# Wider key-value products and denominators in a four-layer attention kernel

## The chip, the cores and the metric

The kernel runs on one core of one Trainium2 chip. The metric is the device time of one execution in microseconds (us). Times below are a median of three runs; the profile is one more execution, read with the hardware profiler.

## The reference

Four residual blocks follow each other on x of 2048 rows by 512 columns: A, B, A, B, the two A with the same weights and the two B as well. Each block normalizes its input, projects it to queries, keys and values of 32 heads with 16 columns each, and ends with a projection by wo. A is attention in a causal window of 256 rows with a softmax; B is linear attention over all rows, whose denominator is one number per row and head.

```python
    def _B_ref(x, wqkv, wo):
...
        phi = lambda t: jnp.where(t > 0, t + 1, jnp.exp(t)) + 1e-6
        pq, pk = phi(q), phi(k)
        kv = jnp.einsum("bhsd,bhse->bhde", pk, v)
        z = jnp.einsum("bhsd->bhd", pk)
        num = jnp.einsum("bhqd,bhde->bhqe", pq, kv)
        den = jnp.einsum("bhqd,bhd->bhq", pq, z)[..., None] + 1e-6
        o = num / den
        return (lambda x, *d: x.transpose(*d))(o, 0, 2, 1, 3).reshape(B, S, D) @ wo

    x = A_x
    x = x + _A_ref(_layernorm(x, axis=-1), A_wqkv, A_wo)
    x = x + _B_ref(_layernorm(x, axis=-1), B_wqkv, B_wo)
    x = x + _A_ref(_layernorm(x, axis=-1), A_wqkv, A_wo)
    x = x + _B_ref(_layernorm(x, axis=-1), B_wqkv, B_wo)
```

## The kernel before

The rows lie in 16 tiles of 128 and in 4 groups I of 4 tiles. The program has two rounds, a = 0 and a = 1, each of one A and one B block. Within a round, group I runs through LayerNorm and transposes (`ln_tile`), the A projections (`prep`: keys, queries, values), scores, exponentials, masks and products with the values (`attention`), the output of A (`out_A`), LayerNorm again, and the B projections (`b_proj`). After the last group, `kv_final` makes what the second half of B needs; that half, `norm_p2`, runs while the next round's A has begun, and for a = 1 it ends the program.

In B each tile's phi(k) and v give a product of 512 columns of phi(k) by 33 columns (32 of v and a 1), split in 16 blocks of 32 rows of the result. `kv_unit` does two tiles at a time: 32 matmuls, each with 32 weight columns, which go to four column groups of the array, into one PSUM bank; VectorE then adds the bank to the running sum `kvs`. The denominators are made by `norm_pair(h)` for two groups I at once: 8 matmuls (L1072) with 64 weight columns from `zc` and 512 moving columns of phi(q), in two column groups of 64; then ScalarE takes Ln and Exp of -1 times that, one engine copies the reciprocals to bf16 (`hl`), and VectorE adds the rest in the other rows. `norm_unit` spreads them to the columns of each head (L1097) and VectorE multiplies phi(q) with them (L1101); `p2_tile` projects with `wkv`, the key-value product already multiplied with wo.

A transpose (`transpose`, L553) is done either on TensorE (four matmuls against the identity, L568, and a copy out of PSUM, L571) or by a DMA from the SP queue (L559). `by_pe` says which. Two sums of check flags (`check_layer`) multiply one column of flags as the weights with a column of ones.

The order of all work is written out by hand in the string `ORDER` (L214): each word is an operation's number, the engine that does it (P TensorE, A ScalarE, V VectorE, G GpSimd, S the SP queue) and the buffers that it takes; the planner emits them in that order. A word such as `9F0` puts matmuls without use into a bank (`fill`, L464) where TensorE would stand idle. Operations whose cost names more than one engine can stand on either; masks, copies out of PSUM, LayerNorm's parts and phi's middle step are of this kind.

```python
        for t in range(NCT):
            k_unit(key, I, t)
            q_unit(key, I, t)
```

For I = 0 the keys and queries come in halves (`k_half`, `q_half`): half 0 needs the transposed tiles 0 and 1, half 1 the tiles 2 and 3.

Of the kernel before, what the change touches and what calls it, by code (L numbers as in the profile page):

```python
# [10 lines left out]
ALU = mybir.AluOpType  # L11
# [208 lines left out]
130P 131P 99V 163P04 344V1 164A 102P3 162G 132V 165A 188P06 638V0 348G 141P4 189A 142P 143P 144P 119S 154P5 103V 166G  # L220
155P 156P 190A 145V 157P 193P02 13G 158V 345P4 194A 340P6 167P7 349V0 168P 639G 169P 346V 170P 195A 171V 199P04 11G
646V1 200A 31S 110P2 12G 355P7 111V 201A 341V 1F3 204P02 192G 650V2 381P6 43S 647G 205A 350P5 382P 351V 203G 206A 356V
198G 210P04 640V12 32H 363P7 383V 30H 641S 211A 364P 209G 191G 365V 212A 2F3 224P02 651G 108P6 172S0 225A 385P4 109V
196G 386P 197G 213V 226A 384S 229P06 207V 202G 387V 214P5 215P 230A 648V1 216P 208G 360P4 652V3 642V0 231A 217P 235P02
361P 653S 218V 643G 236A 357P7 362V 358P 228G 237A 649S 644V0 233G 240P04 359V 219P6 241A 220P 221P 645S 222P 238V 242A
947V0 246P02 389P7 390P 247A 223V 245G 388S 227G 391V 248A 2F5 397P04 232V 234G 239G 1F6 668P7 398A 249V 948G 669P 244V
250P6 392S 399A 670V 402P02 251P 671V 403A 252P 401G 253P 939V1 243G 393P7 404A 407P04 254V 940G 394P 176S1 408A 366P6
395V 367P 943V2 409A 412P02 396S 255P7 368V 256P 413A 944G 257P 258P 411G 682P6 414A 259V 418P04 400G 683P 410V 419A
264S2 416V 661P7 415G 684V 662P 420A 405V 434P02 417G 663V 260S3 369P6 435A 422V 370P 421G 664V 654P5 41S 406G 436A 655P
423V 371V 424P4 439P20 437G 425P 51S 276V 441A 429P6 430P 656V 426P 440A 431P 657V 427P 33S 432P 428V 444P02 372P7 445A  # L230
433V 373P 47S 446A 374V 449P04 378P6 951V3 686P7 450A 447G 34H 49S 687P 448V 952G 438V 451A 941V00 455P02 379P 688V 442G
456A 679P5 37S 380V 454G 680P 453G 443V 457A 452V 471P06 681V 35S 473A 459V 458G 3F4 476P24 460V 953V1 472A 461P7 466P6
689S 462P 477A 474V 467P 475G 463P 468P 478A 464P 36H 469P 465V 481P02 173P5 480G 39S 482A 479V 470V 174P 483A 175V
486P06 375P4 685S 180V1 376P 487A 485G 377V 181G 488A 2F5 492P20 40H 694P5 42H 695P 493A 48H 949V3 489G 50H 954S 945V2
658P7 490V 659P 494A 696V 177P6 942S 491V 508P42 484V 660A 496V 495G 178P 509A 497V 498P7 179V 697S 499P 510A 500P
513P04 184V0 503P6 514A 504P 501P 505P 515A 502V 506P 518P02 507V 261P7 519A 517G 262P 690P6 520A 263V 523P04 691P 511V
524A 265P7 692V 266P 525A 516V 529P02 693S 267V 530A 521V 2F6 665P5 528G 527V 522G 666P 526V 531A 698P06 667V 512G 675P4
185G 950S 699A 676P 532V 534V 533V 677V 700A 2F5 703P20 45S 540P5 268V2 541P 704A 535P7 701V 542P 269G 536P 705A 946S
543P 537P 544V 538P 708P02 706G 539V 672P6 702G 46H 709A 557S0 182G01 44H 673P 678V 52H 38H 710A 674V 713P04 979P7 553S1
980P 714A 711G 976P6 712G 981V 549S2 715A 719P02 270G1 977P 720A 717V 545S3 958P4 718G 959P 978V 721A 716G 955P5 707V  # L240
960V 735P06 956P 737A 723V 722G 982S 724V 957V 730P4 736A 740P62 731P 272V1 732P 741A 725P5 726P 273G 727P 742A 728P
733P 739G 745P60 734V 546P2 744G 746A 729V 554P3 555P 747A 577V 750P64 556V 547P 751A 748G 743V 983P3 548V 984P 752A
756P06 569V2 757A 755G 985V 738G 749V 758A 986S 5F2 772P42 753V 754G 773A 760V 3F1 777P06 759G 761V 8V 778A 767P4 762P5
183S 768P 774A 763P 769P 764P 779A 271S 770P 765P 782P02 766V 961P7 781G 783A 274G2 780V 962P 771V 558P6 784A 963V
787P04 275S 559P 788A 785G 967P3 560V 775G 968P 789A 786V 793P06 776G 991P2 969V 794A 992P 792G 791V 795A 993V 2F5
809P40 790V 810A 797V 2F3 814P26 798G 796V 186G0 561V1 815A 799P5 804P4 800P 811A 562G 805P 187S 801P 806P 816A 802P
813V 563G32 807P 803V 819P02 964P7 820A 808V 570G 965P 550P6 817G 821A 966V 824P04 551P 825A 823V 319P7 822V 320P 552V
826A 830P02 321V 331P6 831A 812V 332P 829G 828V 313P7 827G 333V 832A 314P 995P04 818G 315V 996A 834G 835V 2F6 1000P62
833V 1002A 565V0 836P1 841P0 837P 573V1 997A 842P 838P 843P 1001A 839P 998G 844P 840V 1006P24 566G 322A0 987P7 571V0
846S3 1007A 988P 1005G 845V 325P6 567G1 1008A 989V 326P 1011P02 323V 1003G 970P7 327V 1012A 850S1 574G 971P 973P6 1013A  # L250
972V 1017P04 858S0 974P 324V 1018A 1016G 847P7 975V 1004G 848P 994S 1019A 1031P02 1015G 1014V 282P60 849V 1032A 1020G
283P 878V 859P7 1033A 999G 862V0 1036P04 854S2 860P 1037A 1009V 863G 277P21 861V 1021P3 572S 278P 1038A 1010V 284V 1022P
1026P7 1035V 279A 1023P 1039G 1024P 334A2 575G2 280V 1042P04 1025V 290P61 1043A 281V 1027P 335G 576S 291P 874V1 1044A
1028P 1047P02 1029P 990S 1049A 285P50 336V 286P 1048A 855P4 1030V 856P 292V 864G20 287A 1053P02 851P7 564S 1040V 1054A
288V 852P 1051G 289V 295P62 1055A 568S 296P 875G 857V 293P5 297A 1050V 1034G 1083P02 294V 303P40 1046V 1085A 298V 300P51
1041G 853V 301P 1056G 1084A 299V 304P 1052G 308P70 870V0 302A 1057P6 305A 1088P02 1045V 871G 578P51 1090A 306V 1058P
307V 579P 1089A 872G0 1059P 309P 1060P 310A 1062P4 873S 1061V 1094P02 580A 311P7 1096A 1063P 312V 583P60 866V0 1064P
1095A 584P 581V 1065P 582V 316A0 1099P02 1098G 632P7 1066V 867G 1101A 633P 585V 1067S0 876G3 586P52 1100A 634V 587P
591P41 317V 868G1 588A 1105P02 626P7 589V 1107A 1091V 592P 1102G 869S 318V 627P 1097G 1106A 590V 1068P6 1069P 1092V 865S
# [90 lines left out]
def build(ctx, tc, A_x, A_wqkv, A_wo, B_x, B_wqkv, B_wo, out, force_safe=False):  # L350
# [94 lines left out]
    def fast_network(ctx_f):  # L445
# [62 lines left out]
        for k in range(3):  # L508
            nc.vector.memset(vss[k][:, :, 32:33], 1.0)
# [928 lines left out]
```

## Time and profile before

| | |
|---|---|
| median of 3 runs | 422.84 us (422.48 to 422.93) |
| the profiled execution | 423.23 us |
| its span, first to last instruction | 421.4 us |
| granted TensorE clock, mean | 0.998 |
| instructions | 15390 |

The profiled execution is 1.83 us longer than its span and 0.39 us above the median. In the page, a line's busy time is a union over the instructions of an engine. In the chain of waits, each piece is the time by which that work moved the end on, so a piece can be shorter than the instruction in it; "issue" is time in which the engine waited for nothing that the profile shows.

### The profile page before, as it was taken

The numbers are of one execution on the slowest core, as the hardware profiler recorded it, in microseconds if no ns is written. First come the engines' busy times: TensorE is split into PE (matmuls) and PEld (weight loads), VectorE is DVE, ScalarE is ACT, GpSimd is POOL, SyncE is SP. The second block draws the span as 40 slices with busy tenths as digits, with TensorE's granted clock in tenths as the row PEclk, the third lists the DMA queues.
The fourth block names the chain that finished last, engine by engine and source line by source line (L and its number), as shares of the span: only waits on it lengthen the run. The fifth ranks groups of instructions, "written<-read, shape, count | busy, mean of one in ns | idle before, by whom it ended". The sixth has DMA issues, their size and how long they took to land.

```text
span 421.4 us, 15390 instructions
## 1 busy us (share of the span) xinstructions
PE 398.1 (94%) x6281; PEld 221.1 (52%) x6355; DVE 360.9 (86%) x868; ACT 363.3 (86%) x485; POOL 237.0 (56%) x500
## 2 busy tenths in 40 slices
PE   7989999999999999999999999999999999999994
PEld 3665555555555555643555555555555556564341
DVE  6899898877889897988988999989778799888993
ACT  4999989999999999576998999999999999955630
POOL 4687633363757763353895566675645449433541
PEclk9999999999999999999999999999999999999999
DMA  7333273151203230100022123122213202210023
GB/s 232 119 82 77 66 196 80 38 99 29 40 16 66 52 63 16 29 2 0 5 64 54 39 48 63 42 52 64 52 28 54 52 16 54 39 26 2 2 81 124
DMA packets 64219, 23.86 MB, mean 57 GB/s; under 512 B 45072, under 2 KB 64144, under 8 KB 64144
## 3 DMA queue, kind: packets, MB, share of 16 engines
q1 hardware_dynamic: 62080, 21.38, 23.0%
q10 hardware_dynamic: 2064, 1.44, 1.1%
q8 instruction: 51, 0.84, 0.8%
q14 instruction: 24, 0.20, 0.1%
HBM read 6.29 MB, written 2.10 MB: 20 GB/s over the span
## 4 chain that ended last, share of the span: by engine, by line
PE 52%; ACT 18%; DVE 16%; issue 7%; DMA 2%; POOL 2%; another core or an unknown queue 0%; SPq 0%; DVEq 0%; ACTq 0%; POOLq 0%
PE psb L539 31%; PE psb L882 11%; ACT pt L839 9%; ACT pt L836 7%; PE psb L825 7%; DVE pqT L1101 2%; DVE pt L854 2%; DMA wA<-in_A_wqkv_dram 2%; DVE kall L775 2%; DVE qT L529 1%; DVE kall L790 1%; PE psb L568 1%; POOL pt L859 1%; PE psb L997 1%; DVE o_sb L896 1%
## 5 line engine op out<-in xcount | busy, mean ns | idle before, releaser
L859 POOL TENSOR_SCALAR_AFFINE_SELECT pt<-pt 128x256 bf16<-128x256 bf16 x279 | 116.5, 447 | 101.3 <-ACT pt L839 70.2
L836 ACT ACTIVATE pt<-psb 128x1024 bf16<-128x1024 f32 (+2 forms) x156 | 156.6, 1008 | 9.0 <-PE psb L825 7.8
L839 ACT ACTIVATE pt<-psb 128x1024 bf16<-128x1024 f32 (+2 forms) x156 | 156.6, 1011 | 3.8 <-PE psb L825 1.8
L882 PEld LDWEIGHTS <-pt 128*128 128x128 bf16 x2880 | 83.0, 96 | 19.0 <-issue 5.6
L882 PE MATMUL psb<-vbd,pt 128*128 128x34 bf16 x2880 | 87.5, 178 | 2.5 <-ACT pt L836 0.6
L539 PE MATMUL psb<-xnT,wA 128*128 128x512 bf16 (+1 forms) x306 | 65.3, 335 | 2.1 <-issue 0.5
L825 PE MATMUL psb<-qT,kall 32*128 32x256 bf16 (+4 forms) x1664 | 63.5, 241 | 2.5 <-ACT pt L836 0.8
L539 PE MATMUL psb<-wB,xnT 128*128 128x512 bf16 x230 | 62.0, 379 | 2.1 <-issue 1.1
L854 DVE TENSOR_TENSOR pt<-pt,tri 128x256 bf16<-128x256 bf16 (+1 forms) x138 | 52.7, 404 | 4.3 <-ACT pt L839 3.0
L825 PEld LDWEIGHTS <-kall 32*128 32x128 bf16 x1664 | 28.7, 92 | 47.7 <-issue 43.0
L539 PEld LDWEIGHTS <-xnT 128*128 128x128 bf16 x384 | 32.2, 97 | 35.8 <-issue 6.7
L539 PEld LDWEIGHTS <-wA 128*128 128x128 bf16 x320 | 27.7, 97 | 24.9 <-issue 6.5
L539 PE MATMUL psb<-wA,xnT 128*128 128x512 bf16 x112 | 32.5, 380 | 2.4 <-DMA wA<-in_A_wqkv_dram 0.9
L539 PE MATMUL psb<-woA,oT 128*128 128x512 bf16 x118 | 32.9, 380 | 1.0 <-issue 0.5
L539 PE MATMUL psb<-xnT,wB 128*128 128x512 bf16 x123 | 33.3, 379 | 0.4 <-issue 0.2
L539 PE MATMUL psb<-wkv,pqT 128*128 128x512 bf16 (+1 forms) x129 | 31.0, 373 | 0.9 <-DVE pqT L1101 0.5
L896 DVE TENSOR_TENSOR o_sb<-psb,rall 128x256 bf16<-128x256 f32 x64 | 27.2, 425 | 2.3
L895 DVE RECIPROCAL rall<-psb 128x16 f32<-128x16 f32 x64 | 16.1, 251 | 14.1 <-PE psb L882 11.1
L663 DVE BATCH_NORM_STATS2 ln<-xres 128x6 f32<-128x512 f32 (+1 forms) x39 | 26.6, 682 | 1.3 <-DMA xres<-in_A_x_dram 1.1
L950 ACT ACTIVATE pks<-psb 128x512 bf16<-128x512 f32 x32 | 19.4, 614 | 5.9 <-PE psb L539 5.8
L598 POOL TENSOR_TENSOR ln<-ln,mhalf 128x1 f32<-128x1 f32 x36 | 21.0, 582 | 3.0
L956 DVE SCALAR_TENSOR_TENSOR pks<-psb,pks 128x512 bf16<-128x512 f32 x32 | 22.0, 687 | 0.6
(129 smaller groups left out, 525.4 us busy)
## 6 DMA issues: line engine op xcount, KB each, us to landing
vbd<-vst SPq DMA_DIRECT2D x128, 34.0 KB, 1.9
wB<-in_B_wqkv_dram SPq DMA_DIRECT2D x6, 256.0 KB, 3.8
out_dram<-ost SPq DMA_DIRECT2D x10, 128.0 KB, 2.0
xres<-in_A_x_dram SPq DMA_DIRECT2D x4, 256.0 KB, 3.1
xnT<-xn SPq DMA_TRANSPOSE x48, 2.5
out_dram<-ost ACTq DMA_DIRECT2D x5, 128.0 KB, 1.7
wA<-in_A_wqkv_dram SPq DMA_DIRECT2D x1, 512.0 KB, 7.3
xres<-in_A_x_dram SPq DMA_DIRECT2D x1, 512.0 KB, 8.3
```

The source lines that it names most:

```text
L539: nc.tensor.matmul(t["t"][:], lhsT=lhs(c), rhs=rhs(c), start=(c == 0), stop=(c == NCT - 1))
L598: nc.gpsimd.tensor_tensor(out, out, mhalf[:, 0:1], op=ALU.pow)
L663: nc.vector.bn_stats(t["st"], x())
L825: nc.tensor.matmul(psb[:, sT.k + x if x < 2 else sS.k + x - 2, at * 64:(at + w) * 64], lhsT=kbd[half(m)][32 * x:32 * x + 32, tt, m % 4, :, :],
L836: nc.scalar.activation(body[:, 0:2, 0:w_all, :], psb[:, sT.k:sT.k + 2, 0:w_all * 64].rearrange("p x (s c) -> p x s c", c=64), ACT.Exp, sca ...
L839: nc.scalar.activation(body[:, 2:4, 0:w_all, :], psb[:, sS.k:sS.k + 2, 0:w_all * 64].rearrange("p x (s c) -> p x s c", c=64), ACT.Exp, sca ...
L854: nc.vector.tensor_tensor(v, v, mt, op=ALU.mult)
L859: nc.gpsimd.affine_select(out=v, in_=v, compare_op=ALU.is_ge, fill=0.0, base=1 if kind == 0 else -2, pattern=[[0, 4], [2 * sg, 64]], chann ...
L882: nc.tensor.matmul(t["O"][:, x, g, :, :], lhsT=parts[b][0][:, s0:s0 + 2, :], rhs=vbd[half(m)][:, m % 4, :, 4 * tt + g, :], start=(n == 0), ...
L896: nc.vector.tensor_tensor(o_sb[:, u0:u0 + nu, P * tt:P * tt + P].rearrange("p u (h e) -> p u h e", e=DH), Ov[:, :, :, 0:DH], r.to_broadcas ...
L950: nc.scalar.activation(dst(), ps()[:], ACT.Exp)
L956: nc.vector.scalar_tensor_tensor(out=dst(), in0=ps()[:], scalar=1.0 + 1e-6, in1=dst(), op0=ALU.add, op1=ALU.max)
```

## The change

1. `kv_unit` does four tiles at once (64 matmuls) for I = 0, 1, 2 and two at a time only for I = 3: 10 units in place of 16, of the same 512 matmuls in all, and 10 copies or additions of `kvs` in place of 16. The buffers of phi(k) and v grow from 3 to 5.
2. `zc` gets 32 columns in place of 64; a denominator's 8 matmuls go to four column groups of 32, which can stand in the array at once, two matmuls summed in each.
3. The sums of flags have a column of ones spread to 128 weight columns, and the flags as the moving column.
4. In round a = 1, group 0, tiles 2 and 3 are transposed by DMA and no longer on TensorE.
5. `kvn` and `hl` have no buffers of their own any more and use those of phi(k).
6. One landing time that the order was planned with (`wA`, values) is 9.5 in place of 8.6, and `ORDER` is new as a whole: fills 50 in place of 45, 60 in place of 68 copies by `evac` on VectorE and 32 in place of 24 on ScalarE, 28 in place of 20 LayerNorm applications on VectorE and 11 in place of 19 on GpSimd.

```diff
-7V 3G 6G 1G 14H 53V3 15H 0G 9G 58V2 17H 54A 5G 55V00 2G 59A 68A1 9F0 56P6 60V2 18H 19H 16H 63V0 61P4 57V 62V 64A 3F1
...
-                 "pks": Ring(3), "vs": Ring(3), "ln": Ring(4)}
+                 "pks": Ring(5), "vs": Ring(5), "ln": Ring(4)}
...
-        kvn = fp.tile([P, NCT, P], BF, name="kvn")
-        zc = fp.tile([P, NCT, 2, 2, DH], BF, name="zc")
+        zc = fp.tile([P, NCT, 2, DH], BF, name="zc")
...
-                nc.tensor.matmul(t["p"][:], lhsT=t["ok"][:], rhs=ones_bf[:], start=True, stop=True)
-            o2 = pl.op({"PE": .1}, f2, deps=[o], take=[s])
+                nc.tensor.matmul(psb[:, s.k, 0:1], lhsT=ones_bf[:].to_broadcast([P, P]), rhs=t["ok"][:], start=True, stop=True)
+            o2 = pl.op({"PE": .03}, f2, deps=[o], take=[s])
...
-        def kv_unit(i):
+        def kv_unit(i, tiles):
...
-                        for n in range(2):
+                        for n in range(tiles):
...
-                for c in range(NCT):
+                for n in range(2):
                     for k in range(2):
-                        nc.tensor.matmul(psb[64 * k:64 * k + 64, s.k, :], lhsT=zc[:, c, :, :, :],
-                                         rhs=pqT[:, c, (2 * h + k) * 512:(2 * h + k + 1) * 512],
-                                         start=(c == 0), stop=(c == NCT - 1), tile_position=(0, 64 * k))
+                        for q in range(2):
+                            c, r = 2 * q + n, 64 * k + 32 * q
+                            nc.tensor.matmul(psb[r:r + 32, s.k, :], lhsT=zc[:, c, :, :], rhs=pqT[:, c, (2 * h + k) * 512:(2 * h + k + 1) * 512],
+                                             start=(n == 0), stop=(n == 1), tile_position=(0, r))
...
-                if u % 2:
-                    kv_unit(4 * I + u - 1)
+                if u == 3 and I < NI - 1:
+                    kv_unit(4 * I, 4)
+                elif u % 2 and I == NI - 1:
+                    kv_unit(4 * I + u - 1, 2)
...
-                    ln_tile(ka, 4 * I + u, a == 0, by_pe=I == 0 or I == 1 and a == 0)
+                    ln_tile(ka, 4 * I + u, a == 0, by_pe=I == 0 and (a == 0 or u < 2) or I == 1 and a == 0)
```

Line numbers after the change are 1 lower up to L930, and up to 12 higher from L1041 on. The order moved at these places.

The SP queue at the start of round a = 1, group 0 (the values of its tiles go to `vbd_137` and `vbd_138`). Before:

```order
L559 DMA_TRANSPOSE xnT<-xn 128x4x128 x2
L808 DMA vbd_137<-vst_135 64x272 x4
L808 DMA vbd_137<-vst_136 64x272 x4
L559 DMA_TRANSPOSE xnT<-xn 128x4x128
L808 DMA vbd_138<-vst_135 64x272 x4
```

And now:

```order
L558 DMA_TRANSPOSE xnT<-xn 128x4x128 x5
L807 DMA vbd_137<-vst_135 64x272 x4
L558 DMA_TRANSPOSE xnT<-xn 128x4x128 x2
L807 DMA vbd_137<-vst_136 64x272 x4
L558 DMA_TRANSPOSE xnT<-xn 128x4x128
```

The two transposes between the first and the second group of four scatters are the new ones. On TensorE, 8 fills in a row stand at this place between the third group of scores and the first projection of half 1; there were none.

ScalarE over the same stretch, where the exponentials of round 1 begin (`pt` their outputs, `qT` and `vst` copies out of PSUM). Before:

```order
L836 ACTIVATE pt_148<-psb 128x2x448
L839 ACTIVATE pt_148<-psb 128x2x448
L529 CAST qT_143<-psb 128x256
L836 ACTIVATE pt_149<-psb 128x2x192
L839 ACTIVATE pt_149<-psb 128x2x192
L836 ACTIVATE pt_150<-psb 128x2x448
L839 ACTIVATE pt_150<-psb 128x2x448
```

And now:

```order
L835 ACTIVATE pt_148<-psb 128x2x448
L838 ACTIVATE pt_148<-psb 128x2x448
L528 CAST vst_135<-psb 128x32x16
L528 CAST qT_143<-psb 128x256
L835 ACTIVATE pt_149<-psb 128x2x192
L838 ACTIVATE pt_149<-psb 128x2x192
L835 ACTIVATE pt_150<-psb 128x2x448
L528 CAST qT_143<-psb 128x256
L838 ACTIVATE pt_150<-psb 128x2x448
```

Two copies more stand between the same exponentials. From the first to the last exponential of round 1, ScalarE has these more: two parts of `kall` (L788), two copies to `qT` and two to `vst` of 512 columns, and two pairs of Ln and Exp for LayerNorm (L594, L595); and one square (L614) and one phi exponential (L950) less. In round 0 the numbers are nearly equal.

## Rows read from the trace of the kernel before

**Rows 1.** The page, part 1: busy us (share of the span) xinstructions.
```profile
PE 398.1 (94%) x6281; PEld 221.1 (52%) x6355; DVE 360.9 (86%) x868; ACT 363.3 (86%) x485; POOL 237.0 (56%) x500
```

**Rows 2.** Stages: us, busy us per engine (x instructions), clock, DMA share, GB/s.
```profile
core 0: us, PE busy (x) PEld busy (x) DVE busy (x) ACT busy (x) POOL busy (x), PEclk, DMA share, GB/s
11.10:170.00 158.90, 152.43 (x2697) 88.54 (x2725) 136.29 (x328) 153.55 (x184) 93.60 (x214) 1.00 0.31 68
170.00:209.80 39.80, 38.80 (x427) 20.52 (x432) 35.76 (x94) 28.66 (x61) 21.33 (x24) 1.00 0.04 8
209.80:371.90 162.10, 156.86 (x2729) 88.62 (x2762) 142.90 (x338) 154.50 (x186) 100.17 (x224) 1.00 0.24 48
371.90:412.00 40.10, 38.72 (x380) 18.43 (x384) 36.32 (x79) 20.51 (x41) 15.70 (x16) 1.00 0.10 31
```

**Rows 3.** The chain of waits, 166 to 222 us: start, us, what.
```profile
176.24 0.86 PE psb L539 x4
...
181.21 0.32 PE psb L997 x32
181.53 0.16 issue
...
191.88 0.98 PE psb L1072 x8
...
208.39 0.22 PE psb L568 x4
...
209.79 0.33 PE psb L568 x4
...
216.87 0.98 PE psb L1072 x8
```

**Rows 4.** The chain of waits, 150 to 160 us: the first piece of L997.
```profile
156.57 0.32 PE psb L997 x32
```

**Rows 5.** The chain of waits, 366 to 422 us.
```profile
389.68 0.33 PE psb L997 x32
...
391.88 1.00 ACT pqT L950 x2
...
400.42 0.98 PE psb L1072 x8
...
404.10 0.10 PE psb L934
```

**Rows 6.** Groups by line and shape: xcount | busy us, mean ns | idle before.
```profile
L1004 DVE TENSOR_TENSOR kvs<-psb,kvs 128x132 f32<-128x132 f32 x14 | 4.1, 290 | 1.6 <-PE psb L997 1.5
```

**Rows 7.** The page, part 6: DMA issues xcount, KB, us to landing.
```profile
xnT<-xn SPq DMA_TRANSPOSE x48, 2.5
```

**Rows 8.** Groups by line and shape, ScalarE.
```profile
L788 ACT ACTIVATE kall<-psb,eo 128x256 bf16<-128x256 f32 x8 | 3.6, 552 | 0.0
L529 ACT CAST qT<-psb 128x512 bf16<-128x512 f32 x1 | 0.6, 642 | 0.0
L529 ACT CAST vst<-psb 128x512 bf16<-128x512 f32 x5 | 3.0, 590 | 1.7 <-PE psb L539 1.6
L594 ACT ACTIVATE lrs<-lssq,eps 128x1 f32<-128x1 f32 x5 | 1.5, 292 | 0.5 <-DVE xn L616 0.4
L595 ACT ACTIVATE lrs<-lrs 128x1 f32<-128x1 f32 x5 | 1.0, 203 | 0.2
L614 ACT ACTIVATE xn<-xres,lsum 128x512 bf16<-128x512 f32 x12 | 8.6, 717 | 1.7 <-DVE xres L738 0.9 <-issue 0.7
L950 ACT ACTIVATE pks<-psb 128x512 bf16<-128x512 f32 x32 | 19.4, 614 | 5.9 <-PE psb L539 5.8
```

**Rows 9.** TensorE in order of time at the start: start, us [idle before <-releaser].
```profile
9.58 1.02 PE L539 MATMUL psb<-wA,xnT 128*128 128x512 bf16 x4 [0.92 <-DMA wA<-in_A_wqkv_dram]
```

More of the change, by code (lines that the diff above doesn't have):

```diff
@@ L220 @@
[L220 to L224, printed above, removed]
@@ L486, in fast_network @@
         kvs = fp.tile([P, NCT, 33], F32, name="kvs")
[L487 to L488 removed]
+        zc = fp.tile([P, NCT, 2, DH], BF, name="zc")
         nc.vector.memset(zc[:], 0.0)
[L490 to L492 removed]
+        hl = {}
+        vss = [fp.tile([P, NP, 33], BF, name=f"vs{k}") for k in range(5)]
         wkv = fp.tile([P, NCT, D], BF, name="wkv")
@@ L507, in fast_network @@
             nc.vector.memset(vst[k][:, :, :, DH:VW], 1.0)
-        for k in range(3):
+        for k in range(5):
             nc.vector.memset(vss[k][:, :, 32:33], 1.0)
@@ L985, in bv_unit @@
             kv_in[i].append((t, vs_, f))
-        def kv_unit(i):
-            ins = [kv_in[i + n] for n in range(2)]
+        def kv_unit(i, tiles):
+            ins = [kv_in[i + n] for n in range(tiles)]
             s = bank()
@@ L995, in f @@
                     for g in range(4):
-                        for n in range(2):
+                        for n in range(tiles):
                             nc.tensor.matmul(t["t"][32 * g:32 * g + 32, c, :], lhsT=ins[n][0][0]["t"][:, c * P + 32 * g:c * P + 32 * g + 32],
-                                             rhs=ins[n][1][0]["t"][:, 4 * c + g, :], start=(n == 0), stop=(n == 1), tile_position=(0, 32 * g))
-            o = pl.op({"PE": .228}, f, deps=[x[2] for y in ins for x in y] + B("kvs").r + B("kvs").w, use=[x[1] for y in ins for x in y], take=[s], kind="kv")
+                                             rhs=ins[n][1][0]["t"][:, 4 * c + g, :], start=(n == 0), stop=(n == tiles - 1), tile_position=(0, 32 * g))
+            o = pl.op({"PE": .114 * tiles}, f, deps=[x[2] for y in ins for x in y] + B("kvs").r + B("kvs").w, use=[x[1] for y in ins for x in y], take=[s], kind="kv")
             def fe(e):
@@ L1035, in kv_final @@
         def kv_final():
+            ks = slot("pks")
+            kt = {}
+            kvn = lambda: kt["t"][:].rearrange("p (t c) -> p t c", c=P)
+            first = []
             for jj in range(2):
@@ L1096, in f @@
                     r = 64 * (I % 2) + 32 * n
-                    nc.tensor.matmul(t["p"][:, n, :], lhsT=spread[r:r + 32, j, :, :], rhs=hl[I // 2][r:r + 32, :], start=True, stop=True,
+                    nc.tensor.matmul(t["p"][:, n, :], lhsT=spread[r:r + 32, j, :, :], rhs=held["h"][r:r + 32, :], start=True, stop=True,
                                      tile_position=(r, 0))
-            o = pl.op({"PE": .235}, f, reads=[B("hl", I // 2)], take=[s], kind="rows")
+            o = pl.op({"PE": .235}, f, reads=[B("hl", I // 2)], take=[s], use=[hs], kind="rows")
             def f_m(e):
```

291 lines of the change are left out of this document (151 added, 140 removed).

## The prediction, written before the change was run

> **What bounds the kernel now.** I read the page first, then the stages, then the chain of waits, then the groups by line. The page puts TensorE at 94% of the span and ScalarE and VectorE at 86% each [rows 1], but those are means over stages with different limits, and the stages tell them apart [rows 2]. From the first to the last exponential of round 0 (11.1 to 170.0 us) ScalarE is busy 153.55 of 158.90 us, so it idles 5.35 us or 3.4%; in round 1 (209.8 to 371.9) it is busy 154.50 of 162.10 and idles 7.60 or 4.7%. TensorE idles about as little there (6.47 and 5.24 us), and either can hold the other. In the two stretches between, 170.0 to 209.8 and 371.9 to 412.0, ScalarE is busy 28.66 of 39.80 and 20.51 of 40.10 us, while TensorE is busy 38.80 and 38.72: there TensorE sets the pace. The chain says the same: from 176 to 217 us its pieces are those of TensorE, and among them stand the very pieces that the change touches [rows 3]. So an edit that shortens TensorE's work pays in the two stretches between, less where exponentials run; and work that is put on ScalarE costs nothing between and may cost in round 1.
>
> **The change, part by part.**
>
> Denominators. Four times 8 matmuls of 512 columns. Three of the four lie on the chain with 0.98 us each [rows 3, 5]: both of round 0 (191.88, 216.87) and the second of round 1 (400.42). The fourth, at 391.8, is not on it: two phi exponentials on ScalarE end last there [rows 5], and Ln of the denominators stands behind such exponentials in the new order too, so I count nothing for it. Four full matmuls take 0.86 us on the chain, 0.215 each [rows 3]; 8 in 0.98 are therefore two at a time, with 0.12 for going in and out. No row shows four groups of 512 moving columns. Bounds: 0.98 again (no gain) and 0.49 (half). The nearest row is the one of the same matmuls, where two groups did run at once, so I take half: **3 x 0.49 = -1.47 us**. [...]
>
> Key-value products. The same 512 matmuls in 10 units in place of 16. A unit of 32 takes 0.32 us on the chain and is followed by 0.16 of "issue" before full-width work goes on [rows 3]. Of the 16 units 12 lie on the chain, the first at 156.57 and the last at 389.68 [rows 4, 5]. Of a unit that is merged away its matmuls remain; what goes is the entry and the exit. Bounds for one: 0, and 0.48 if 64 cost no more than 32. I take the 0.16, which the row gives: 6 x 12/16 x 0.16 = **-0.72 us** (0 to -2.16). VectorE loses 6 additions of 0.29 us [rows 6]; they are not on the chain, and I count them at nothing; in the stretches between VectorE has about 4 us to spare in 40 [rows 2]. A later product keeps four tiles of phi(k) and v waiting; the five buffers cover that.
>
> Two transposes. Tiles 2 and 3 of group 0 in round 1 are on the chain with 0.22 and 0.33 us [rows 3]: **-0.55 us** and two copies out of PSUM. In their place the SP queue gets two transposes, each 2.5 us to landing [rows 7]; they stand between the scatters of two tiles' values, and a queue that waits for LayerNorm holds the second group of scatters back. These feed products that come after eight groups of scores, and have time. What waits for the transposes themselves is half 1 of keys, queries and values of that group. The order has 8 fills there, that is 8 x 0.215 = 1.72 us in which it gives TensorE nothing better. If ScalarE works on exponentials meanwhile this costs 0; if TensorE holds the end, as it does now between 209 and 217, all of it. The exponentials of half 0 need no half 1, which speaks for cover; the chain, which runs through TensorE there, speaks against. I take half: **+0.86 us** (0 to 1.72).
>
> Flag sums. The one on the chain takes 0.10 [rows 5]; with full width I take 0.03: **-0.07** (0 to -0.10).
>
> Engines. In round 1 ScalarE gets, by the durations of its rows [rows 8], 2 x 0.552 + 2 x 0.642 + 2 x 0.590 + 2 x (0.292 + 0.203) = 4.56 us more and 0.717 + 0.614 = 1.33 less: 3.23 us. Bounds: 0, when the 7.60 us of idle take it, and +3.23. Round 0 shows that such a stage can run with 3.4% idle [rows 2]; at that share 162.1 us leave 5.5, so 2.1 fit and 1.1 do not. I take half of that, **+0.55 us**, since VectorE is relieved by the same copies.
>
> Start. Values wait for `wA` there, 0.92 us on TensorE [rows 9]. A zero fill of 2176 columns moves from GpSimd to ScalarE ahead of the first LayerNorm. By the copies of 512 columns (0.590, [rows 8]) it is bounded by 0.6 and 4 x 0.590 = 2.4. The first projections get later by about as much as the wait is long, and the values still start when the weights land. Counted at nothing; if the cover is short, up to 1 us is lost.
>
> Masks and LayerNorm parts that change between VectorE and GpSimd I count at nothing, as neither sets the chain for long in any stage.
>
> **The sum:** -1.47 - 0.72 - 0.55 - 0.07 + 0.86 + 0.55 = -1.40. The profiled execution took 423.23 us, so 421.83; it was 0.39 above the median of 422.84, hence **421.4 us**. With the lower bounds (-2.16 for the merged units, -0.10 for the flags, nothing for fills and ScalarE) the sum is -4.28, which gives 418.6; the forecast's own range is 418.6 to 422.6.
>
> **Rivals.**
>
> *ScalarE takes over round 1.* Two copies now stand between the exponentials at its start. If the idle time of 7.60 us is waiting that no copy can fill, all 3.23 us lengthen that stage, and what TensorE saves in it (the denominator at 216.87, the two transposes, about a third of the merged units) is worth nothing. What stays is 2 x 0.49 + 0.48 + 0.07 = 1.53; the fills lie under ScalarE. 423.23 - 1.53 + 3.23 = 424.93, less 0.39: 424.5 us. For it speaks 95% busy in the stage; against it that round 0 lived with less idle. It decides from about 2.1 us of copies on that find no gap. Chance 0.16.
>
> *Four column groups don't run at once.* Then the denominators keep 0.98 us, and the sum is +0.07: 422.9 us. For it: only the key-value products use four groups now, and 32 matmuls of 33 columns in 0.32 us are 10 ns each, where 33 columns at 0.215 us per 512 are 14 ns: some overlap, not four at once. Against it: those are small, so that something else may pace them. Chance 0.10. [...]
>
> *The gains are swallowed:* the fills lie fully on the path (+1.72) and merging saves nothing (0), without a cost on ScalarE. -1.47 - 0.55 - 0.07 + 1.72 = -0.37: 422.5 us. For it speaks the length of that run of fills, the longest behind the start. Chance 0.16.
>
> **How the numbers follow.** The forecast has 0.58. The range 418.6 to 424.3 takes it, both rivals near no change and the lower half of the ScalarE rival, and leaves out some 0.15. A measurement of this kernel can tell about 0.2% from no change, 0.85 us, so the bounds are 422.0 and 423.7. Faster: nearly all of the forecast and little of the others, 0.56. Same: the two rivals near 422.7 and the forecast's upper end, 0.26. Slower: the ScalarE rival, and a start that loses its cover, 0.18.
>
> **What would show it.** Right: denominators' pieces of about 0.5 us on the chain; TensorE's share of the two stretches between unchanged and the stretches shorter by 0.5 to 1.5 us each; ten pieces of key-value products with fewer "issue" gaps; round 1 between its first and last exponential no longer than 162.5 us, with ScalarE idle nearer to 5 us. Wrong: denominators of 0.9 us; the fills of round 1 on the chain with "DMA xnT" behind them; ScalarE over 96% busy in round 1 with a longer stage; the first exponential later than 11.5 us.

## The result, and the profile after

The kernel after the change takes **426.32 us** (median of five executions, 425.88 to 428.42; a sixth of 887.84 us is left out and its cause is not known). With that sixth the median is 426.40, the figure that the expectations below quote. The kernel before, run beside it, took 423.02 us. The ratio is 1.0085, with an interval from 1.0066 to 1.0103: slower by 3.3 us, where 1.4 us less was forecast. Run a second time (below), it came out at 1.0060 (1.0039 to 1.0081).

The page of the profiled execution (426.32 us, span 424.5) says little of it. TensorE is as busy as in [rows 1]:

```profile
PE 397.3 (94%) x6277; PEld 221.7 (52%) x6352; DVE 361.3 (85%) x865; ACT 369.4 (87%) x497; POOL 227.3 (54%) x482
```

So I cut the execution at its own marks: the start of the first and the end of the last exponential of each round, the end of the last matmul, the end of the span. The view of stages, after the change, with the columns of [rows 2]:

```profile
11.20:170.32 159.12, 150.52 (x2684) 87.73 (x2710) 137.34 (x332) 152.37 (x184) 87.20 (x203) 1.00 0.33 69
170.32:209.59 39.27, 38.17 (x415) 19.41 (x419) 33.96 (x82) 29.60 (x64) 19.73 (x25) 1.00 0.03 5
209.59:373.15 163.56, 157.90 (x2710) 90.70 (x2745) 145.35 (x343) 156.63 (x192) 96.03 (x210) 1.00 0.25 48
373.15:416.51 43.36, 41.84 (x427) 20.02 (x432) 37.81 (x79) 23.51 (x45) 17.73 (x19) 1.00 0.12 36
416.51:424.50 7.99, 0.00 (x1) 0.00 (x0) 0.69 (x1) 0.00 (x0) 0.00 (x0) 0.67 0.35 113
```

The stage behind the last matmul in the kernel before:

```profile
415.17:421.43 6.26, 0.00 (x0) 0.00 (x0) 0.72 (x2) 0.00 (x0) 0.00 (x0) 0.86 0.35 113
```

The same marks in the kernel before, and in the runs that follow, give this table (us, from the order-of-time view of each profile; "whole" is the median of all executions, and the ratio is to the kernel before in the same session):

| | first exponential | round 0 | between | round 1 | to the last matmul | after it | whole | ratio (interval) |
|---|---|---|---|---|---|---|---|---|
| before | 11.12 | 158.85 | 39.87 | 162.09 | 43.23 | 6.26 | 423.02 | |
| **after** | 11.20 | 159.12 | 39.27 | 163.55 | 43.37 | **7.99** | 426.32 | 1.0085 (1.0066-1.0103) |
| e11, after again | 11.27 | 158.87 | 39.27 | 163.93 | 43.36 | 8.08 | 426.10 | 1.0060 (1.0039-1.0081) |
| e3, more TensorE instructions | 11.11 | 158.49 | 39.27 | 163.53 | 43.37 | 6.02 | 423.77 | 1.0026 (1.0014-1.0037) |
| e1, no fills in round 1 | 10.94 | 158.81 | 39.26 | 164.03 | 43.37 | 6.31 | 424.66 | 1.0047 (1.0031-1.0063) |
| e2, transposes on TensorE | 11.11 | 158.26 | 39.27 | 166.39 | 43.37 | 6.59 | 427.90 | 1.0125 (1.0093-1.0157) |
| e6, the same, copies on VectorE | 10.94 | 158.03 | 39.27 | 164.19 | 43.37 | 8.47 | 426.16 | 1.0069 (1.0044-1.0095) |
| e7, less on ScalarE | 11.66 | 158.28 | 39.28 | 164.99 | 43.75 | 5.79 | 426.68 | 1.0090 (1.0065-1.0114) |
| e8, later statistics | 10.94 | 158.68 | 39.28 | 163.58 | 43.37 | 6.41 | 424.78 | 1.0047 (1.0028-1.0067) |
| e10, no fills in the tail | 11.71 | 158.21 | 39.26 | 164.02 | 44.70 | 6.36 | 423.94 | 1.0009 (0.9992-1.0025) |
| e4, denominators alone | 10.69 | 159.28 | 39.86 | 161.63 | 44.38 | 6.20 | 423.37 | 1.0006 (0.9994-1.0019) |
| e5, e4 and three fills | 10.53 | 159.26 | 39.87 | 161.64 | 45.41 | 5.71 | 424.39 | 1.0022 (1.0007-1.0037) |
| e9, the same, free bank | 11.41 | 159.12 | 39.87 | 162.01 | 42.85 | 5.65 | 422.46 | 0.9976 (0.9966-0.9987) |
| e12, e9 and a step moved | 10.04 | 158.80 | 39.41 | 161.96 | 42.84 | 5.81 | 421.57 | 0.9972 (0.9961-0.9984) |

From before to after, the span gains 0.08 + 0.27 - 0.60 + 1.46 + 0.14 + 1.73 = 3.08 us. Two stages hold it: **round 1, and the time after the last matmul**; my sum had no term for the second. Between runs with the same order the stretch between the rounds and the one to the last matmul repeat to some hundredths. Round 0 scatters by up to 1.1 us, round 1 by half a us, the first exponential by 0.8, and the time after the last matmul has a cause of its own, shown below. In the five runs with the whole order of round 1 as after the change (after, e11, e3, e8, e10) the 149th of the 156 exponentials starts 153.96 to 154.00 us behind the first: all of that round's scatter lies behind it.

The chain of waits after the change, at the places of [rows 3, 5]:

```profile
182.77 0.76 PE psb L996 x56
...
213.29 1.83 PE psb L464 x8
...
382.34 0.70 PE psb L996 x50
383.04 0.16 issue
...
393.51 0.55 PE psb L1079 x8
394.06 0.75 PE psb L464 x3
...
396.98 0.43 PE psb L464 x2
```

The denominators do run four groups at once, 0.55 us in place of 0.98. But in the tail, the stretch to the last matmul, matmuls without use (L464) stand behind them on the chain with 1.18 us, and the 8 fills of round 1 are on it with their full length.

After the last matmul both kernels write the last output tiles. In the kernel after, a packet of code comes in between (queue q8; I take it for TensorE's, since its 51 packets make one for some 250 TensorE instructions). The DMA view from 420.1 to 421.9 us: queue, packets, MB, share of the 16 DMA engines:

```profile
q1 hardware_dynamic: 132, 0.12, 19.4%
q8 instruction: 1, 0.02, 5.7%
```

One packet of 16 KB takes 5.7% of 16 x 1.8 us, 1.64 us of one DMA engine (it starts at 420.18). The same view from 420.6 us to the end, in 40 slices of 0.0975 us:

```profile
GB/s 0 0 84 0 0 0 0 0 0 0 0 0 11 11 11 11 11 11 0 21 0 0 0 0 0 0 0 0 0 0 0 0 0 0 0 0 0 0 0 0
DMA packets 10, 0.02 MB, mean 4 GB/s; under 512 B 1, under 2 KB 9, under 8 KB 9
```

All of the output has landed by 420.56 us but eight rows of 1 KB, which start when the packet of code has ended (421.82, the 13th slice) and come in one after another until 422.55. That they were queued on the packet's own DMA engine is inferred from these times. The program ends 1.95 us later. In the kernel before the last data came at 419.36, 4.2 us behind the last matmul, and the end 2.07 behind it.

### The profile page after: what moved, and what is told of

Its sections match the earlier page's. It is cut to its first block, busy times and chain, and to the rows that moved or that the text cites. A ratio compares the mean times of both kernels' runs of the same rounds, so it can differ in the third digit from the quotient of the medians.

```text
span 424.5 us, 15368 instructions
## 1 busy us (share of the span) xinstructions
PE 397.3 (94%) x6277; PEld 221.7 (52%) x6352; DVE 361.3 (85%) x865; ACT 369.4 (87%) x497; POOL 227.3 (54%) x482
## 4 chain that ended last, share of the span: by engine, by line
PE 59%; DVE 17%; ACT 11%; issue 5%; POOL 3%; DMA 3%; SPq 0%; ACTq 0%; DVEq 0%; POOLq 0%
PE psb L538 35%; PE psb L881 13%; PE psb L824 7%; ACT pt L838 6%; ACT pt L835 5%; DMA xres<-in_A_x_dram 3%; DVE pt L853 3%; DVE kall L774 2%; DVE kall L789 2%; DVE pqT L1111 1%; DVE ln L662 1%; PE psb L996 1%; PE psb L464 1%; POOL pks L952 1%; PE psb L1107 1%
## 5 line engine op out<-in xcount | busy, mean ns | idle before, releaser
L858 POOL TENSOR_SCALAR_AFFINE_SELECT pt<-pt 128x256 bf16<-128x256 bf16 x277 | 114.8, 444 | 99.7 <-ACT pt L838 72.4
L881 PE MATMUL psb<-vbd,pt 128*128 128x34 bf16 x2880 | 86.4, 178 | 2.9 <-ACT pt L838 1.2
L538 PEld LDWEIGHTS <-xnT 128*128 128x128 bf16 x384 | 33.4, 97 | 36.4 <-issue 4.4
L538 PE MATMUL psb<-xnT,wB 128*128 128x512 bf16 x118 | 32.3, 380 | 0.8 <-issue 0.3
```

Of the source, the lines that this page charges most:

```text
L538: nc.tensor.matmul(t["t"][:], lhsT=lhs(c), rhs=rhs(c), start=(c == 0), stop=(c == NCT - 1))
L858: nc.gpsimd.affine_select(out=v, in_=v, compare_op=ALU.is_ge, fill=0.0, base=1 if kind == 0 else -2, pattern=[[0, 4], [2 * sg, 64]], chann ...
L881: nc.tensor.matmul(t["O"][:, x, g, :, :], lhsT=parts[b][0][:, s0:s0 + 2, :], rhs=vbd[half(m)][:, m % 4, :, 4 * tt + g, :], start=(n == 0), ...
```

## The experiments

e1, e2, e3, e6, e7, e8 and e10 each change one place of the kernel after. e4 changes the kernel before, e5 and e9 add fills to e4, and e12 adds one moved step to e9.

**e3: where TensorE's code packets fall.**

```diff
         def fill(k, n):
+            if n == 11:
+                for _ in range(24):
+                    nc.tensor.matmul(psb[:, k, 0:256], lhsT=identb[:], rhs=identb[:].unsqueeze(1).to_broadcast([P, 2, P]), start=True, stop=True)
+                return
             for _ in range(n):
```

> The kernel after with 24 fills of 256 columns in place of the first 11 of 512, while TensorE waits for the first LayerNorm anyway: 26 more TensorE instructions, so the last regular 16 KB packet of its code is asked for about 31 instructions before its end in place of 5. Code theory (this packet and the one after it come too late; the second, 420.18 to 421.82 us, holds up eight packets of the last output until 422.54): time after the last matmul falls from 7.99 us to 6 to 6.5 as before the change, and the whole from 426.4 to 424.4 to 424.9. Output theory (more of the output is written at the end, and the check's result comes later, matmul at 412.87 in place of 404.10): stays at 7.7 to 8.2, and the whole within 0.4 of 426.4.

Measured: 6.02 us after the last matmul, 423.77 us (0.6 under the range expected), ratio 1.0026. The DMA view from 410.80 to 415.77 us has the packet that came after the last matmul before:

```profile
q8 instruction: 1, 0.02, 1.1%
```

The code theory holds, and gives more than half of the loss. The rest of the table row is that of the kernel after, within the scatter of the stages.

**e11: the kernel after once more.** No edit.

> The kernel after, unchanged, on the chip of these runs. Code theory: the last regular packet of TensorE's code again within 10 instructions of its end and the time after the last matmul over 7 us, the whole at 426.0 to 426.8, 1.6 to 2.6 over the runs with more or fewer TensorE instructions (423.77 and 424.66). Rival (those two were faster for the chip or the hour they ran in): the whole at 423.8 to 424.9 here.

Measured: 426.10 us, 8.08 us after the last matmul. The DMA view from the last matmul (416.70) to the end, in slices of 0.2 us, has the same thin trail of rows (5 10 10 10 5), and two packets of code again:

```profile
GB/s 355 408 175 20 142 362 347 325 69 68 51 10 15 142 380 157 25 274 345 122 360 198 81 0 0 0 5 10 10 10 5 0 0 0 0 0 0 0 0 0
...
q8 instruction: 2, 0.03, 1.9%
```

So it belongs to the program, not to a chip or an hour. Over all 14 profiles: where a regular packet came before the last matmul (or none was due, e1 and e10), the time after it was 5.65 to 6.41 us. Where it came 0.3 us behind it, the packet that follows started 3.7 to 4.5 us behind the last matmul, and the time was 7.99, 8.08, 8.47 where that fell among the last rows, 6.59 and 5.79 (e2, e7) where they were all but through. What decides when the packet is asked for is not settled: e8 has the same TensorE instructions as the kernel after, in the same order, and asked 31 of them earlier. So e3 shows that the place of the packet matters, not that the number of instructions alone sets it.

**e1: no fills in round 1.**

```diff
-1561G 8F5 1309P5
+1561G 1309P5
```

> The kernel after without the 8 fills ahead of the first projection of half 1 in round 1. Fills theory (TensorE is held there by work without use, 1.83 us on the chain of waits): the projection starts near 213.3 us in place of 214.96 and round 1, first to last exponential, goes from 163.56 to 161.8 to 162.4. Landing theory (the second of the two transposes by DMA, issued at about 212.15 us, lands 2.3 to 2.4 later, at about 214.5): TensorE waits for the DMA instead, the projection starts at about 214.5, and round 1 loses 0.3 to 0.6 at most. ScalarE theory (its extra work sets the end of round 1): the start of half 1 may move, the end of round 1 by no more than 0.2. Apart from that, TensorE has 16 instructions less (8 matmuls, 8 weight loads): if the time after the last matmul hangs on where the last 16 KB packet of TensorE's code falls, it is not 7.99 us but 6 to 6.5.

Measured: TensorE in order of time (start, us, [idle before <-releaser]):

```profile
214.07 1.03 PE L538 MATMUL psb<-xnT,wA 128*128 128x256 bf16 x8 [1.36 <-DMA xnT<-xn]
```

The landing theory's wait: without the fills TensorE waits 1.36 us for the transposes, and starts half 1 at 5.06 us behind the first exponential in place of 5.37. Round 1 got no shorter (164.03): at the 13th exponential e1 is 0.31 us ahead of the kernel after (11.68 against 11.99 us behind the first), at the 149th level with it (153.94 against 153.97). So the fills, or the wait that they cover, cost nothing by then. With 16 TensorE instructions less no regular packet of code was due at the end, an estimate from the some 250 instructions a packet, and the time after the last matmul fell to 6.31; that is where the 1.7 us come from.

**e2 and e6: the two transposes back on TensorE,** in place of the fills; in e2 with one of the two copies on ScalarE, in e6 with both on VectorE (operations behind them are renumbered).

```diff
-by_pe=I == 0 and (a == 0 or u < 2) or I == 1 and a == 0)
+by_pe=I == 0 or I == 1 and a == 0)
-8F5
+1281P5 1282V 1276P2 1277A
```

> The kernel after with the two transposes back on TensorE (8 matmuls, one copy on VectorE, one on ScalarE) in the place of the 8 fills; TensorE has as many instructions as the kernel after. Landing theory: the first projection of half 1 starts at about 214.1 (0.44 of matmuls and a copy of 0.4 to 0.6) in place of 214.96, and round 1 is 0.7 to 1.2 shorter than 163.56. Fills theory: the same start, since the fills are gone. ScalarE theory: one more copy of 0.56 on ScalarE, so round 1 stays within 0.3 of 163.56. Time after the last matmul: 7.99 us again if the place of TensorE's code decides it.

Measured in e2: round 1 takes 166.39 us, 2.8 longer. The copy stood behind two exponentials on ScalarE; TensorE waited, and then ran 12 matmuls at half clock (0.50 over 216 to 218 us). TensorE in order of time, then the stages 214 to 218 us (the third number from the right is the granted clock):

```profile
214.73 1.87 PE L538 MATMUL psb<-xnT,wA 128*128 128x256 bf16 x8 [1.84 <-ACT xnT L570]
```

```profile
214.00:216.00 2.00, 1.27 (x7) 0.87 (x7) 0.69 (x3) 0.68 (x2) 1.75 (x4) 0.69 0.36 83
216.00:218.00 2.00, 2.00 (x7) 0.85 (x6) 1.77 (x3) 0.00 (x0) 1.83 (x5) 0.50 0.00 0
```

The same 8 matmuls took 1.03 us in e1, where TensorE had waited 1.36 us at full clock. None of the theories had this.

> The kernel after with the two transposes on TensorE in place of the 8 fills, and both copies on VectorE, ahead of the two squares of LayerNorm: the copy that waited on ScalarE behind two exponentials (TensorE idle 1.84 us, then 12 matmuls at half clock) is gone. Hole theory (round 1 loses at its start what TensorE waits there): the first projection of half 1 starts 4.1 to 4.5 us after the first exponential in place of 5.37, no half clock, round 1 162.2 to 162.8 in place of 163.55, the whole 425.0 to 425.8 against 426.40. ScalarE theory (its extra work sets round 1): round 1 163.2 to 163.8, the whole 426.1 to 426.7. The time after the last matmul stays at 6.6 to 8 us.

Measured in e6: half 1 starts 4.86 us behind the first exponential, not at the 4.1 to 4.5 expected, the clock stays full (1.00 over 210 to 220 us), and still round 1 takes 164.19 us, the whole 426.16. The 13th exponential of the round is 0.4 us earlier than in the kernel after (11.56 against 11.99 us from the first), the 37th no longer (37.50 against 37.31). (The expectations call these the 12th and the 36th, counted from 0.) So what TensorE waits or fills ahead of half 1 does not make round 1 as long as it is: the hole theory falls in that form. The opening of the round as a whole is another matter (below).

**e7: less on ScalarE in round 1.**

```diff
-1577A ... 1583A ... 1606A ... 1906A ... 1789A ... 2315A
+1577V ... 1583V ... 1606V ... 1906V ... 1789G ... 2315G
```

> The kernel after with work of round 1 moved off ScalarE at its place in the order: three copies of 512 columns and one part of the keys to VectorE, two pairs for LayerNorm to GpSimd: about 4 us less on ScalarE, about 2.7 more on VectorE, 1.7 more on GpSimd. ScalarE theory: round 1 is 1 to 2 us shorter than 163.55, the whole 424.4 to 425.4 against 426.40. Hole theory (the start of round 1 sets it, at 5.37 us for the first projection of half 1): round 1 within 0.3 of 163.55, or longer by up to 1 if VectorE comes late instead.

Measured: round 1 is 1.44 us longer (164.99), the whole 426.68. The gain that the ScalarE theory expected did not come. This alone does not refute it, since the moved work may cost more where it went than it did on ScalarE; the rows of round 1 below do.

**e8: later statistics at the start.** The two words `335V0 336G` move down, to just ahead of `350V1`.

> The kernel after with the LayerNorm statistics of row tile 4 (VectorE waits 2.85 us for its transfer, until 12.86) put behind the copies of the values, of the third transposed tile and the first keys that stood behind it. Theory of the start: the 12th exponential comes 1 to 2 us earlier (after: 10.5 us behind the first; before: 9.2). Absorbed (ScalarE and VectorE catch up over round 0, as they did in the kernel after, 1.6 us behind at the 48th exponential and 0.35 at the end): round 0 ends within 0.4 of 169.4 to 170.3 and the whole within 0.5 of 426.40. Rival (the lost time of the start is in the result): the whole is 1 to 1.6 faster.

In the kernel after, VectorE stood still for a transfer of x; in e8 the copy of the values that was behind it starts 1.5 us earlier (VectorE in order of time, the kernel after, then e8):

```profile
12.86 0.69 DVE L662 BATCH_NORM_STATS2 ln<-xres 128x6 f32<-128x512 bf16 x1 [2.85 <-DMA xres<-in_A_x_dram]
```

```profile
12.17 0.69 DVE L528 CAST vst<-psb 128x512 bf16<-128x512 f32 x1 [2.15 <-PE psb L538]
```

The 13th exponential comes 10.07 us behind the first. That is 0.4 earlier than in the kernel after (10.47), but five other runs without the edit (e11, e3, e1, e2, e10) have 10.01 to 10.12, and e6 9.38: the edit did not bring it forward, so the theory of the start fails. The whole is 424.78, and nearly all of that gain is in the time after the last matmul (6.41).

**e4: the denominators alone,** in the kernel before: `zc` with 32 columns and the four-group loop of the change.

> The kernel before with the denominators in four column groups of 32 and nothing else: order, fills, transposes and key-value products as before. Prediction's term: the pieces of 8 denominator matmuls fall from 0.98 to 0.49 to 0.55 us and three of four lie on the chain: 1.3 to 1.5 faster, 421.5 to 421.8. Rival (what TensorE gains is waited for on ScalarE's Ln and Exp or VectorE's products behind it): 0 to 0.6 faster, 422.4 to 423.0.

Measured: 423.37 us, ratio 1.0006 (0.9994 to 1.0019), outside both ranges. No gain, though the pieces are 0.55 us. The chain of waits of its profiled execution shows two reasons:

```profile
190.84 2.07 POOL pks L1029
192.92 0.08 issue
193.00 1.27 POOL kvn L1048 x2
194.27 0.04 issue
194.31 0.29 PE psb L568 x2
...
397.97 3.56 PE psb L539 x10
401.53 0.55 PE psb L1074 x8
```

Between the rounds the transposes (L568) wait for the masked products (`kvn`), which GpSimd makes behind a step of phi; they start at 194.31. In the kernel before the same transposes start at 194.27, behind the denominators and six projections:

```profile
192.87 1.40 PE psb L539 x6
194.27 0.35 PE psb L568 x4
```

So GpSimd's work was hidden behind TensorE's there with nothing to spare, and the stretch stays at 39.86 us. In the tail 10 projections take 3.56 us that took 1.91 before, at a lower clock. Stages of e4, then of the kernel before:

```profile
395.00:400.00 5.00, 4.27 (x17) 1.45 (x18) 5.00 (x8) 2.28 (x5) 1.92 (x1) 0.80 0.00 0
400.00:405.00 5.00, 4.84 (x25) 1.71 (x25) 4.04 (x7) 2.97 (x5) 1.27 (x1) 0.86 0.10 31
```

```profile
395.00:400.00 5.00, 4.38 (x23) 1.44 (x22) 5.00 (x8) 2.82 (x6) 1.92 (x1) 1.00 0.00 2
400.00:405.00 5.00, 4.84 (x30) 1.77 (x29) 4.66 (x9) 3.00 (x5) 1.85 (x2) 1.00 0.19 61
```

TensorE's idle time in the stretch ahead is 0.28 us longer in e4 (it comes earlier to the row spreading, and VectorE is not ready). The granted clock is 0.80 and 0.86 over these stages of 5 us, against 1.00 in the kernel before. That it stood at half in between is an estimate: 0.50, as e2 had it over 216 to 218 us, for 2.0 and 1.4 us gives these two means, and 3.4 us is nearly the length of the 10 projections (3.56).

The half clock explains this execution, not the median. Three of e4's 12 executions, the profiled one among them, have a mean granted clock of 0.991 or 0.992; the other nine have 0.995 to 0.999, as the kernel before had beside it, and their median is 423.14 us, no faster either. What takes the gain of the tail there is not shown.

**e5 and e9: e4 with three fills more in the tail.** In e5 the two single fills went into bank 7, in e9 into bank 5.

```diff
-2F7 2508P3 ... 2531P3 ... 2510P7
+3F7 2508P3 ... 1F5 2531P3 ... 1F5 2510P7
```

> The kernel before with the denominators in four column groups (as in the run with that alone) and three matmuls without use more, in the tail where TensorE waits for the norm's products: 3 in place of 2 ahead of the first row spreading (L1098), one ahead of the third, one ahead of the first projection with wkv. Clock theory (with the denominators alone, TensorE's granted clock stood at half over the 10 projections at 397.97 to 401.53 us, 3.56 us in place of 1.91, after a stretch with four idle pieces): the clock stays full, the 10 projections take 1.9 to 2.0, the tail is 42.5 to 42.9 us in place of 44.38, and the whole 421.6 to 422.2 against 423.37 for the denominators alone. Rival (the half clock has another cause): the tail stays over 44 and the whole at 423.2 to 423.6.

Measured in e5: 424.39 us, the tail 45.41. A mistake of mine: a product of VectorE was still reading bank 7, and the fill made the wait longer that it was to bridge; the granted clock fell again (0.86 over 395 to 400 us, 0.80 over 400 to 405). TensorE in order of time:

```profile
397.81 0.38 PE L464 MATMUL psb<-identb 128*128 128x512 bf16 x1 [1.48 <-DVE pqT L1102]
```

> The kernel before with the denominators in four column groups and the same three matmuls without use more as in the last try, but the two single ones into a bank that nothing reads at that time (there they went into one that a product of VectorE was still reading, and the first stood 1.48 us behind it). Clock theory (with the denominators alone the clock falls to half because TensorE idles more in the stretch ahead of it): full clock from 395 to 405 us, the 10 projections with wkv in 1.9 to 2.0 us in place of 3.56, the tail 42.5 to 43.0 in place of 44.38, the whole 1.2 to 1.8 under the denominators alone, 421.6 to 422.3. Rival (the half clock has another cause, or the fills delay the products): the tail stays over 44, the whole at 423.2 or more.

Measured in e9: **422.46 us, ratio 0.9976** (0.9966 to 0.9987), faster than the kernel before. The clock is full (0.996 or more in all 11 executions), the 10 projections take 1.91 us, the tail 42.85:

```profile
395.00:400.00 5.00, 4.91 (x24) 1.66 (x23) 4.74 (x7) 3.23 (x7) 2.39 (x2) 1.00 0.01 2
400.00:405.00 5.00, 4.94 (x33) 1.78 (x31) 4.93 (x10) 2.98 (x5) 1.88 (x2) 1.00 0.19 63
```

The tail gains 0.38 us over the kernel before, one denominator on the chain, and 1.53 over e4's profiled execution. More of what e9 gains over the kernel before lies behind the last matmul (5.65 against 6.26 us), where the place of the code packets counts (7.99 us in the kernel after, 6.02 in e3): that part is not the denominators'.

**e10: the kernel after without its 5 fills in the tail** (`3F2` and `2F7` taken out).

> The kernel after without its 3 and 2 fills in the tail (394.06 and 396.98 us on the chain of waits, 0.75 and 0.43 us). Clock theory (they hold the clock over the wait for the norm's products): without them the granted clock falls to half between 395 and 405 us, as with the denominators alone, and the tail is 1 to 2 us longer than 43.37. Rival (they only fill a wait, or stand in the way): tail 42.9 to 43.4, clock full. TensorE has 10 instructions less, so the last packet of its code may fall past the end: time after the last matmul 6 to 6.5 in place of 7.99.

Measured in the profiled execution: the mean clock falls to 0.67 over 400 to 405 us, 6 projections take 2.74 us that took 1.47 in e11, and the tail is 44.70 us.

```profile
400.00:405.00 5.00, 4.99 (x23) 1.77 (x24) 4.21 (x6) 1.24 (x2) 0.00 (x0) 0.67 0.00 0
```

So without the fills the clock can fall, as the theory had it, but it does not in most executions. The 12 lie from 422.50 to 426.41 us; the two longest, the profiled one (425.99) among them, have a mean granted clock of 0.991 and 0.992, the ten others 0.996 to 0.999. The whole is 423.94 us, with 6.36 us after the last matmul.

**e12: e9 with one step of phi on VectorE.**

```diff
-919G
-1234V
+1234V 919V
```

> The faster kernel (before, denominators in four column groups, three matmuls without use more in the tail) with one middle step of phi of round 0 on VectorE (0.28 us) in place of GpSimd (2.07 us), behind the two zc. With the denominators alone the stretch between the rounds kept its 39.87 us, and the chain there ran through that step, the masked key-value products behind it on GpSimd (L1048, until 194.27) and their transposes on TensorE. Theory (TensorE's 0.43 us at the denominators were worth nothing there because the transposes waited for GpSimd): the stretch falls from 39.87 to 39.4 to 39.6 us, the whole from 422.46 to 422.0 to 422.3. Rival (the reciprocals, ready on VectorE at about 196.4, hold the products anyway): the stretch within 0.1 of 39.87, the whole within 0.2 of 422.46.

Measured: the stretch between the rounds takes 39.41 us, as expected, and the denominators are back on the chain, with 0.55 us:

```profile
168.84:208.25 39.41, 38.85 (x434) 20.32 (x433) 36.57 (x95) 28.72 (x62) 19.31 (x23) 1.00 0.05 8
```

```profile
190.75 0.55 PE psb L1073 x8
```

The whole is 421.57 us, below the 422.0 to 422.3 expected, ratio 0.9972 (0.9961 to 0.9984). Against e9 the stage shows the gain, the ratios alone would not tell the two apart. It is the fastest kernel here.

**Round 1, without a run of its own.** The records of matmuls in the profiles of before and after are incomplete (6281 of 6355, 6277 of 6352, by the weight loads), so idle times of TensorE are compared in two that are whole: e9 for the old order, e8 for the new. Round 0 of each:

```profile
11.41:170.53 159.12, 155.25 (x2726) 88.43 (x2723) 136.20 (x327) 153.58 (x184) 93.28 (x214) 1.00 0.32 68
```

```profile
10.94:169.61 158.67, 152.53 (x2711) 87.54 (x2710) 137.36 (x332) 152.32 (x184) 87.78 (x203) 1.00 0.32 69
```

TensorE idles 3.87 us there in the old order, 6.14 in the new, in small waits for VectorE and ScalarE (3.8 to 4.0 and 5.7 to 6.3 over all whole profiles); it does 2.7 us less in the round, and has 8 more of the B projections left when it ends (36 matmuls of `xnT` with `wB` from there to the 37th exponential of round 1, 28 in e9). In that stretch of the new order TensorE idles 0.8 of 76.6 us. From the first exponential to the last matmul the new order has 394.4 us of work for TensorE and 10.5 of idle time, e9 396.3 and 7.5.

The stages of round 1 show where it is lost: from its first exponential to the 13th, to the 37th, and to the 149th. In e9, the old order:

```profile
210.41:219.62 9.21, 8.79 (x99) 4.43 (x98) 8.71 (x21) 8.87 (x18) 8.70 (x11) 1.00 0.24 57
219.62:245.93 26.31, 25.81 (x416) 14.41 (x415) 23.78 (x53) 24.00 (x31) 16.28 (x41) 1.00 0.26 50
245.93:362.64 116.71, 115.02 (x2085) 63.89 (x2085) 101.96 (x244) 112.73 (x131) 68.04 (x159) 1.00 0.25 48
```

In e11, the kernel after:

```profile
209.40:221.39 11.99, 11.84 (x116) 6.42 (x116) 10.04 (x20) 9.66 (x18) 10.19 (x17) 1.00 0.32 75
221.39:246.70 25.31, 25.25 (x418) 14.75 (x417) 23.70 (x57) 24.50 (x31) 12.31 (x32) 1.00 0.26 44
246.70:363.37 116.67, 114.05 (x2099) 64.57 (x2098) 102.18 (x240) 113.83 (x134) 69.50 (x155) 1.00 0.26 48
```

The opening is 2.78 us longer, and TensorE is busy through it while ScalarE idles 2.33 us in place of 0.34. The next stretch gives back 1.00. In the long rest ScalarE does 1.10 us more and the stretch is no longer: its idle time takes that work, and the ScalarE theory falls. So round 1 loses in its opening, on TensorE. The carried projections fit this; that they are the cause, and not the new order of the opening itself, no run isolated.

## Why the prediction was wrong

The forecast was 421.4 us, and the result lies above the range.

- **Missing in the sum: what follows the last matmul.** I took that time as given; it grew by 1.73 us. e3, e11 and the two DMA views show why. The code came in 51 packets of 16 KB, one for some 250 instructions of TensorE, and in the kernel after the last of them took one DMA engine from 420.18 to 421.82 us, ahead of the last eight rows of the output. The program branches past its fallback while that output is being written; that the late packet is the branch's is a guess that no run shows.
- **Denominators, -1.47: the size was right, the place was not.** The pieces are 0.55 us, not the 0.49 that I took. But "three on the chain" does not mean three that pay. Between the rounds GpSimd's products were ready just as late: nothing. In round 1: the 13th exponential comes 0.07 us sooner than before (9.21 against 9.28, e4 and e9), the 37th 0.01 sooner: nothing. In the tail 0.38 in e9's profile, where the clock holds, and 1.15 longer in e4's, where it doesn't (the 10 projections 1.65 longer). The fourth, counted at nothing, was not tried apart. This is the step that failed within the sum.
- **Key-value products, -0.72.** 64 matmuls take 0.70 us with the same 0.16 behind them, against twice 0.48: 0.10 saved for each merged pair, and five are on the chain: 0.5 us, by the pieces. It was not tried alone.
- **Transposes -0.55, fills +0.86.** The fills lay on the chain whole (1.83 us), as the rival of swallowed gains had it. What they cover is the landing of the transposes (1.36 us of waiting in e1), which I had put down to fills. By the 149th exponential neither shows (e1). I looked for the price of the new opening in these pieces; it is 2.7 us longer than before, and round 1 took 163.55 us where I had no more than 162.5.
- **Tail.** One denominator and the flag sum should have made it at least 0.56 us shorter; it is 0.14 longer. Its 5 fills stand on the chain with 1.18 us. Which part of the new order took the gain is open.
- **ScalarE, +0.55,** and the rival that it takes over round 1: its time (424.5) came nearest of those named, but by luck; its mechanism fell with the rows of round 1. ScalarE's busy time there rose by 2.13 us, not 3.23.
- **Start, counted at nothing.** The first exponential moved by 0.08 us only, as I said, but what I did not look at was VectorE's order behind it: a wait of 2.85 us for x, and up to 1.6 us lost by the 49th exponential. By the end of round 0 that is made up (159.12 against 158.85 us, within the scatter), and e8, with the wait moved, started no faster than other runs. What is left is about 2 us more of idle time of TensorE over the whole of round 0.
- **The range.** With the upper bounds of its own terms (0 for the units and the flags, 1.72 for the fills, 3.23 for ScalarE, the rest as summed) the sum is +2.93 and the forecast 425.8 us; the range stopped at 424.3 without a reason in the sum.
- **Four column groups don't run at once,** a rival: they do, by the 0.55 us of the 8 matmuls, against 0.98 in two groups.

The forecast weighed savings by whether their piece stood on the chain. New orders were counted as the old one with pieces taken out and put in. The work did go, but idle time came in its place, and nothing in my sum could show that.

## What to carry to other kernels

A piece on the chain of waits pays only by the slack of the chain beside it: look at what TensorE meets next, when that was ready before, and move that too (e12). Where TensorE's work is shortened ahead of a wait, keep it busy there with matmuls into a bank that nobody reads: without them the mean clock was low (0.991 or 0.992) in 3 of 12 executions of e4 and 2 of 12 of e10, with them in none of 11 of e9. A profile shows one execution; compare its mean clock with the others before a half clock is taken for the cause of a median. When a change of a few tenths of a per cent is judged, compare the time after the last matmul by itself first: it moved by 2 us with the place of a packet of code, not with the work.

## What the runs showed of the hardware that I had not expected

- A packet of 16 KB of code held a DMA engine for 1.64 us, and eight rows of output of 1 KB came only when it had ended. The time after the last matmul was 7.99 us with this and 6.02 without (e3).
- Four column groups of 32 weight columns with 512 moving columns run at once: 8 matmuls in 0.55 us, against 0.98 in two groups.
- In the profiled executions a wait of 1.36 us left the clock full (1.00 over 212 to 216 us, e1); it was halved behind one of 1.84 us (0.50 over 216 to 218 us, e2), and, by the estimate above, behind three waits of 0.27 to 0.35 us (e4), two of which the kernel before has as well, at full clock. Half clock then lasted for 12 and 10 matmuls. In most executions of e4 the mean clock shows no such fall.
